# A transformer-block kernel's first row block: first loads, an early split on ScalarE and GpSimd, and another first order of the products

## The chip, the cores and the metric

The kernel runs on one core of a Trainium2 chip. The metric is the device time of one execution in microseconds (us). Each core has a matrix engine (TensorE, PE in the profile, with its weight loads as PEld), a vector engine (VectorE, DVE), a scalar engine (ScalarE, ACT), a general engine (GpSimd, POOL) and a queue engine that issues DMAs (SyncE, SP).

## The reference, cut to what matters

```
x: 2048 x 640;  w1: 640 x 1536;  w2: 1536 x 640
xn = (x - mean(x)) / sqrt(var(x) + 1e-5)          # by row
a, b = xn @ dft_hid_re.T, xn @ dft_hid_im.T
A = dft_seq_re @ a - dft_seq_im @ b               # 2048 x 2048 matrices
B = gelu(xn @ w1 + b1) @ w2 + b2
out = x + A + B
```

All data are float32. The change touches only the start of B for the first 512 rows: the layer norm, the transposition of the normalized rows, and the first products with `w1`.

## The kernel before

The work goes in four blocks of 512 rows (`TB`), each of four chunks of 128 rows (`NC` = 4), and the hidden dimension of 1536 in twelve chunks of 128 columns (`NF`). The input dimension of 640 makes five pieces of 128 (`ND`, index `j`).

Every float32 operand of a product is split in two float32r parts: a high part, which is a rounded copy that ScalarE writes (`high`, line 186), and a low part, which is the difference that VectorE writes (`low`, line 189). A product of two split operands is three matmuls: high by high, high by low and low by high. `split` (lines 176 to 183) makes both parts.

`hidden(g)` (lines 308 to 323) computes one chunk of the hidden layer for one block: fifteen matmuls into one PSUM bank, a step (j, k) for each of the five pieces `j` and three kinds `k`. Kind 0 is high by high, kind 1 takes the high part of `W1` with the low part of the rows (`XT`), and kind 2 takes the low part of `W1` with the high part of the rows. The first chunk (g = 0) takes its steps in the order of the list `FIRST`; the second (g = 1) has its kind 2 steps last.

The schedule is written out by hand: each engine runs its instructions in the order of the program. There is no planner. Loads go through the queue of SP in that order too; an instruction in that queue that waits holds back those behind it. Tiles of one tag share a few places (`bufs=3` for `w1r` and `w2r`), so that a load waits until the last reader of the tile that held its place is done.

The start of the kernel, in program order:

- SP loads the four row chunks (`load_x`, line 208), then chunks 0 and 1 of `w1` (`load_w1`, line 278, four DMAs each), then chunk 2 of `w1`, chunk 0 of `w2` (`load_w2`, line 285), the bias `b1c`, and chunks 1 and 2 of `w2`.
- VectorE fills three tiles `warm` with zeros, and PE runs 19 matmuls on them into a bank that is not read (`NWARM`, line 666). The three tiles share the places of `w1r`, so the first loads of `w1` wait for the matmuls that read the tile.
- The four chunks are normalized in different ways. Chunk 0: VectorE takes mean and variance (lines 215 and 216), ScalarE the root (690), VectorE the reciprocal and one step of Newton's method (700 to 702, 708, 709), and ScalarE writes the normalized chunk (714). Chunk 1 (`last`): ScalarE takes mean and square sum (692 to 699) and scales it at the end (721). Chunks 2 and 3: VectorE takes the statistics, ScalarE one root for chunks 1 to 3 (707), VectorE the steps behind it (710 to 713), and VectorE normalizes (236) in two pieces for each chunk: columns of pieces 0 and 1, then of 2 to 4.
- ScalarE makes the high part of the first `w1` chunk (723) and VectorE its low part (734).
- PE transposes 20 squares of 128 x 128 into five banks `tacc` (682): those of chunk 0, then pieces 0 and 1 of chunks 2 and 3, all of chunk 1, and the rest; the last one stands behind the first product.
- ScalarE and VectorE split each of the five banks into `XT[j]` (186 and 189).
- PE runs the rest of `hidden(0)`, then `hidden(1)`, which needs the second `w1` chunk (`prep_w1(1)`), and goes on with further chunks and with the products with `w2` (lines 300 to 302).

Of the kernel before, what the change touches and what calls it, by code (L numbers as in the profile page):

```python
# [10 lines left out]
F32 = mybir.dt.float32  # L11
F32R = mybir.dt.float32r
AF = mybir.ActivationFunctionType
ALU = mybir.AluOpType

P = 128
Q = 4
B = 32
EPS = 1e-5
NWARM = 19  # L20
NGATE = (7, 10)
TAIL = 4
PADL = 8
# [3 lines left out]
def kernel(  # L27
# [45 lines left out]
    nc = tc.nc  # L73
    x = x.flatten_outer_dims()
    out = out.flatten_outer_dims()
    S, D = x.shape
    F = w1.shape[1]
    TB = 512
# [3 lines left out]
    ND = D // P  # L82
# [4 lines left out]
    NC = TB // P  # L87
# [4 lines left out]
    def pool(name, side="left", stack=ctx):  # L92
        return stack.enter_context(tc.tile_pool(name=name, bufs=1, side=side, reuse_waits="tile"))
# [22 lines left out]
    def bank(k):  # L116
        return banks[:, k]
# [4 lines left out]
    b1c = const.tile([P, NF], F32, name="b1c")  # L122
    b2c = const.tile([P, ND], F32, name="b2c")
    eps = const.tile([P, 2], F32, name="eps")
    MV = const.tile([P, 4, 6], F32, name="mv")
# [6 lines left out]
    early = pool("early", stack=es_e)  # L132
# [18 lines left out]
    slots = {}  # L151
# [33 lines left out]
    def high(h, s):  # L185
        nc.scalar.activation(h, s, AF.Copy)  # L186
# [17 lines left out]
    def load_x(c, eng=nc.sync, k=None, home=None):  # L204

        slot[c] = c % NC if k is None else k
        xt[c] = (row_places if home is None else home)[:, slot[c]]
        eng.dma_start(xt[c], x[c * P : (c + 1) * P])  # L208

    def ln_stats(c):  # L210
        m = MV
        st = ST[c % 2]
        half = D // 2
        for h in range(2):
            nc.vector.bn_stats(st[:, h, :], xt[c][:, h * half : (h + 1) * half])  # L215
        nc.vector.bn_aggr(m[:, slot[c], 0:2], st.rearrange("p a b -> p (a b)"))  # L216
# [37 lines left out]
    def zo_tile(name, shape=(P, NB, DQ), dtype=F32):  # L254
        return out_pool.tile(list(shape), dtype, tag="zo", bufs=1, name=name)
# [8 lines left out]
    W1, W2, w1r, w2r = {}, {}, {}, {}  # L264
# [4 lines left out]
    def load_w1(i, eng=nc.sync):  # L269

        if i >= 3 * NF:
            return
        f0 = (i % NF if i < 2 * NF else AGAIN[i - 2 * NF]) * P
        t = early.tile([P, ND, P], F32, tag="w2r" if i == NF + 5 else "w1r", bufs=3, name=f"w1r{i}")
        w1r[i] = t
        v = w1.rearrange("(q c i) f -> q i c f", q=Q, i=B)
        for q in range(Q):
            eng.dma_start(t[q * B : (q + 1) * B], v[q, :, :, f0 : f0 + P])

    def load_w2(i, eng=nc.sync):  # L280
        if i >= NF:
            return
        t = early.tile([P, D], F32, tag="w2r", bufs=3, name=f"w2r{i}")
        w2r[i] = t
        eng.dma_start(t, w2[i * P : (i + 1) * P, :])

    def prep_w1(i, n=None):
        if i < NF:
            W1[i] = slots[1, i]
            split(W1[i][:, 0], W1[i][:, 1], w1r.pop(i if n is None else n).rearrange("p a b -> p (a b)"))  # L290

    def prep_w2(i):
        if i < NF:
            W2[i] = slots[2, i]
            split(W2[i][:, 0], W2[i][:, 1], w2r.pop(i), perm=True)
# [12 lines left out]
    def hidden(g, part=slice(None)):  # L308
        i = g % NF
        acc = bank((5 if g < NF else 0) + g % 3)  # L310
        kinds = ((0, 0), (0, 1), (1, 0))
        steps = [(j, k) for j in range(ND) for k in range(3)]
        if g == 0:
            steps = FIRST
        if g == 1:

            steps.sort(key=lambda s: s[1] == 2)
        for n, (j, k) in list(enumerate(steps))[part]:
            a, b = kinds[k]
            nc.tensor.matmul(  # L320
                acc, W1[i][:, a, j * P : (j + 1) * P], XT[j][:, b], start=n == 0, stop=n == len(steps) - 1
            )
        return acc
# [24 lines left out]
        low(hs[:, 1], a, hs[:, 0])  # L348


    FIRST = [(0, 0), (0, 2), (1, 0), (1, 2), (0, 1), (2, 0), (2, 2), (1, 1), (3, 0), (3, 2)]
    FIRST += [(2, 1), (4, 0), (4, 2), (3, 1), (4, 1)]

    def gelu(g, acc, fill=lambda k: None):

# [290 lines left out]

    zeros = rows.tile([P, TB], F32, tag="yt", bufs=2, name="zeros")

    warms = [early.tile([P, TB], F32R, tag="w1r", bufs=3, name=f"warm{k}") for k in range(3)]

    for c in range(NC):
        load_x(c)
    nc.gpsimd.memset(eps, EPS)
    make_identity(nc, ident)
    nc.vector.memset(zeros, 0.0)
# [1 line left out]
        nc.vector.tensor_copy(warm, zeros)  # L657

    nc.scalar.activation(eps[:, 1:2], eps[:, 0:1], AF.Sqrt)
    load_w1(0)  # L660
    load_w1(1)

    wacc = bank(5)
    for k in range(NWARM):
        warm = warms[sum(k >= n for n in NGATE)]
        nc.tensor.matmul(wacc, warm[:, :P], warm, start=True, stop=True)
    load_w1(2)
    load_w2(0)
    nc.sync.dma_start(b1c, b1.rearrange("(i p) -> p i", p=P))
    load_w2(1)  # L670
    load_w2(2)

# [5 lines left out]
    xp = zo_tile("xp", (P, NC, D))  # L678

    def transpose_x(c, j0, j1):  # L680
        for j in range(j0, j1):
            nc.tensor.transpose(tacc[j][:, c * P : (c + 1) * P], xp[:, c, j * P : (j + 1) * P], ident)  # L682
# [4 lines left out]
    f, m = MV[:, 0], MV[:, last]  # L687
# [9 lines left out]
        bias=m[:, 5:6],  # L697
# [2 lines left out]
    nc.vector.reciprocal(root, root)  # L700
    nc.vector.scalar_tensor_tensor(step, root, -0.5, root, op0=ALU.mult, op1=ALU.mult)
    nc.vector.scalar_tensor_tensor(step, f[:, 1:2], EPS, step, op0=ALU.add, op1=ALU.mult)
    for c in (2, 3):
        ln_stats(c)
    others = MV[:, 1:NC]
    v, r, t = others[:, :, 1], others[:, :, 3], others[:, :, 4]
    nc.scalar.activation(r, v, AF.Sqrt, bias=eps[:, 0:1])  # L707
    nc.vector.scalar_tensor_tensor(root, step, 1.5, root, op0=ALU.add, op1=ALU.mult)  # L708
    nc.vector.scalar_tensor_tensor(shift, f[:, 0:1], -1.0, root, op0=ALU.mult, op1=ALU.mult)
    nc.vector.reciprocal(r, r)  # L710
    nc.vector.scalar_tensor_tensor(t, r, -0.5, r, op0=ALU.mult, op1=ALU.mult)
    nc.vector.scalar_tensor_tensor(t, v, EPS, t, op0=ALU.add, op1=ALU.mult)
    nc.vector.scalar_tensor_tensor(r, t, 1.5, r, op0=ALU.add, op1=ALU.mult)
    nc.scalar.activation(  # L714
        chunked(xp[:, 0]),
        xt[0].rearrange("p (q c i) -> p q c i", q=Q, i=B),
# [1 line left out]
        bias=shift,  # L718
        scale=root,
    )  # L720
    nc.scalar.activation(xp[:, last], xp[:, last], AF.Copy, scale=m[:, 3:4])
    W1[0], first_w1 = slots[1, 0], w1r.pop(0).rearrange("p a b -> p (a b)")
    nc.scalar.activation(W1[0][:, 0], first_w1, AF.Copy)

    for j0, j1 in ((0, 2), (2, ND)):
        for c in (2, 3):
# [4 lines left out]
    transpose_x(last, 0, ND)  # L731
    transpose_x(2, 2, ND)
    transpose_x(3, 2, ND - 1)
    nc.vector.tensor_tensor(W1[0][:, 1], first_w1, W1[0][:, 0].bitcast(F32), op=ALU.subtract)
    for j in range(ND):
        split(XT[j][:, 0], XT[j][:, 1], tacc[j])
        if j == 0:
            hidden(0, slice(0, 1))
            transpose_x(3, ND - 1, ND)
# [6 lines left out]
    A["rows_a"] = rows_in("rt2")  # L746
    for c in range(NC, 2 * NC):
        load_x(c, home=A["rows_a"])
    acc0 = hidden(0, slice(1, None))
    prep_w1(1)  # L750
    acc1 = hidden(1)
    prep_w2(0)
    prep_w1(2)
    load_w2(3)
# [937 lines left out]
    for kind, what in stages:  # L1692
        b = blocks.index(what) if kind == "s" else b
# [24 lines left out]
    t = blocks[-2][1]  # L1718
# [38 lines left out]
```

## Time and profile before

| | us |
|---|---|
| median of 3 runs | 852.09 |
| lowest and highest of them | 851.99, 852.13 |
| span of the profiled execution | 849.94 |

The profiled execution's own time is not recorded beside its span; the median stands 2.15 us above the span.

| engine | busy us | share of the span | instructions |
|---|---|---|---|
| PE | 841.9 | 99% | 3711 |
| PEld | 696.7 | 82% | 3711 |
| DVE | 686.7 | 81% | 909 |
| ACT | 368.6 | 43% | 527 |
| POOL | 67.7 | 8% | 116 |

Times in the trace are us from the start of the span. Busy time counts the stretches in which an instruction of the engine runs; matmuls overlap one another, so their starts, not their lengths, give the pace. A row such as `11.03 2.56 ACT L186 ... x5` tells that five instructions of line 186 ran on ScalarE one after another from 11.03 for 2.56 us. A lower-case q behind an engine's name (SPq) is its queue of DMA issues.

### The profile page before, as it was taken

The numbers are of one execution on the slowest core, as the hardware profiler recorded it, in microseconds if no ns is written. First come the engines' busy times: TensorE is split into PE (matmuls) and PEld (weight loads), VectorE is DVE, ScalarE is ACT, GpSimd is POOL, SyncE is SP. The second block draws the span as 40 slices with busy tenths as digits, with TensorE's granted clock in tenths as the row PEclk, the third lists the DMA queues.
The fourth block names the chain that finished last, engine by engine and source line by source line (L and its number), as shares of the span: only waits on it lengthen the run. The fifth ranks groups of instructions, "written<-read, shape, count | busy, mean of one in ns | idle before, by whom it ended". The sixth has DMA issues, their size and how long they took to land.

```text
span 849.9 us, 10599 instructions
## 1 busy us (share of the span) xinstructions
PE 841.9 (99%) x3711; PEld 696.7 (82%) x3711; DVE 686.7 (81%) x909; ACT 368.6 (43%) x527; POOL 67.7 (8%) x116
## 2 busy tenths in 40 slices
PE   8999999999999999999999999999999999999997
PEld 7888888888888888888888888888888888888886
DVE  7979889767844778979978887889967998885687
ACT  7655666654453555443444344232323433323241
POOL 0440024222301000000000000000000000000002
PEclk9999999999999999999999999999999999999999
DMA  8995667878977897958744679763745799705464
GB/s 230 288 248 158 139 163 250 260 223 305 262 192 199 333 323 138 209 120 193 158 137 107 167 220 283 165 144 99 214 150 156 229 237 234 303 19 180 124 172 108
DMA packets 199141, 166.53 MB, mean 196 GB/s; under 512 B 61648, under 2 KB 170192, under 8 KB 198576
## 3 DMA queue, kind: packets, MB, share of 16 engines
q1 hardware_dynamic: 188320, 140.42, 62.7%
q0 software_dynamic: 7600, 24.91, 8.7%
q10 hardware_dynamic: 3168, 0.52, 0.3%
q8 instruction: 29, 0.48, 0.2%
q14 instruction: 24, 0.20, 0.1%
HBM read 115.75 MB, written 46.14 MB: 190 GB/s over the span
## 4 chain that ended last, share of the span: by engine, by line
PE 98%; DMA 1%; DVE 0%; ACT 0%; SPq 0%; issue 0%; ACTq 0%
PE banks L301 29%; PE banks L302 29%; PE banks L300 29%; PE banks L320 10%; DMA row<-in_A_x_dram 1%; PE banks L682 0%; DVE st L215 0%; ACT xp L714 0%; SPq L208 0%; DVE yo L1722 0%; DVE mv L216 0%; ACT mv L707 0%; DVE mv L708 0%; ACTq L707 0%
## 5 line engine op out<-in xcount | busy, mean ns | idle before, releaser
L186 ACT ACTIVATE as<-r 128x1024 fp32r<-128x1024 f32 x80 | 85.0, 1062 | 171.1 <-PE banks L302 150.4
L300 PE MATMUL banks<-as,xab 128*128 128x512 f32 x407 | 158.3, 389 | 0.0
L302 PE MATMUL banks<-as,xab 128*128 128x512 f32 x407 | 158.3, 389 | 0.0
L301 PE MATMUL banks<-as,xab 128*128 128x512 f32 x407 | 158.3, 389 | 0.0
L189 DVE TENSOR_TENSOR as<-r,as 128x1024 fp32r<-128x1024 f32 x80 | 97.2, 1215 | 38.1 <-ACT as L186 38.0
L301 PEld LDWEIGHTS banks<-as,xab 128*128 128x128 f32 x407 | 76.4, 188 | 15.9
L302 PEld LDWEIGHTS banks<-as,xab 128*128 128x128 f32 x407 | 76.4, 188 | 15.8
L300 PEld LDWEIGHTS banks<-as,xab 128*128 128x128 f32 x407 | 76.4, 188 | 15.8
L300 PE MATMUL banks<-as,xc 128*128 128x512 f32 x224 | 87.1, 389 | 0.0
L301 PE MATMUL banks<-as,xc 128*128 128x512 f32 x224 | 87.1, 389 | 0.0
L302 PE MATMUL banks<-as,xc 128*128 128x512 f32 x224 | 87.1, 389 | 0.0
L186 ACT ACTIVATE as<-rt 128x1024 fp32r<-128x1024 f32 x32 | 34.0, 1063 | 72.5 <-PE banks L302 57.9
L320 PE MATMUL banks<-xt,xab 128*128 128x512 f32 x240 | 56.8, 390 | 0.0
L189 DVE TENSOR_TENSOR hs<-ab,hs 128x512 fp32r<-128x512 f32 x36 | 24.7, 685 | 37.6 <-ACT hs L186 37.6
L320 PEld LDWEIGHTS banks<-xt,xab 128*128 128x128 f32 x240 | 45.0, 188 | 9.4
L301 PEld LDWEIGHTS banks<-as,xc 128*128 128x128 f32 x224 | 42.1, 188 | 8.8
L302 PEld LDWEIGHTS banks<-as,xc 128*128 128x128 f32 x224 | 42.0, 188 | 8.7
L300 PEld LDWEIGHTS banks<-as,xc 128*128 128x128 f32 x224 | 42.1, 188 | 8.7
L1280 POOL DMA_DIRECT2D out_dram<-u x4 | 2.6, 658 | 568.8 <-DVE u L463 568.8
L302 PE MATMUL banks<-hs,xc 128*128 128x512 f32 x120 | 46.7, 389 | 0.0
L300 PE MATMUL banks<-hs,xc 128*128 128x512 f32 x120 | 46.7, 389 | 0.0
L301 PE MATMUL banks<-hs,xc 128*128 128x512 f32 x120 | 46.7, 389 | 0.0
(240 smaller groups left out, 1678.9 us busy)
## 6 DMA issues: line engine op xcount, KB each, us to landing
raw<-in_A_dft_seq_re_dram SPq DMA_DIRECT2D x64, 256.0 KB, 5.4
raw<-in_A_dft_seq_im_dram SPq DMA_DIRECT2D x64, 256.0 KB, 5.1
w1r<-in_B_w_dram SPq DMA_DIRECT2D x144, 80.0 KB, 3.5
wit<-wst POOLq DMA_DIRECT2D x15, 384.0 KB, 4.2
wit<-wst POOLq DMA_DIRECT2D x20, 256.0 KB, 4.5
forms_ab<-xab SPq DMA_DIRECT2D x4, 1280.0 KB, 7.7
xab<-wit SPq DMA_DIRECT2D x13, 384.0 KB, 4.5
row<-xn SPq DMA_DIRECT2D x14, 320.0 KB, 5.3
```

Of the source, the lines that this page charges most:

```text
L186: nc.scalar.activation(h, s, AF.Copy)
L189: nc.vector.tensor_tensor(l, s, h.bitcast(F32), op=ALU.subtract)
L300: nc.tensor.matmul(acc, wh, mh, start=first, stop=False, skip_group_check=goes_on)
L301: nc.tensor.matmul(acc, wh, ml, start=False, stop=False, skip_group_check=goes_on)
L302: nc.tensor.matmul(acc, wl, mh, start=False, stop=last, skip_group_check=goes_on)
L320: nc.tensor.matmul(acc, W1[i][:, a, j * P : (j + 1) * P], XT[j][:, b], start=n == 0, stop=n == len(steps) - 1)
L1280: queues[q % len(queues)].dma_start(rows_of(out, t)[:, :, q * DQ + c0 : q * DQ + c1], src[q * B : (q + 1) * B])
```

## The change

- The three `warm` tiles take the places of `w2r`, so that no load of `w1` waits for them, and the loads of `w1`'s chunks 0 to 2 are issued right behind the rows. The bias is loaded ahead of `w2`. One warm matmul less runs (18).
- Chunk 0's last two VectorE steps and ScalarE's write of it stand ahead of the statistics of chunks 2 and 3.
- ScalarE makes the high part of the first `w1` chunk ahead of the scaling of chunk 1.
- GpSimd, and not VectorE, makes the low part of the first `w1` chunk. Ahead of it stands a GpSimd copy of one column of chunk 3's normalized rows into `eps[:, 1:2]`, which nothing reads afterwards; it waits for the last of VectorE's normalizing instructions.
- The list `FIRST` has the first kind 2 step in seventh place and not in second. The second chunk's steps are sorted by kind: all of kind 0, of kind 1, of kind 2.
- The last two steps of the first chunk, (3, 1) and (4, 1), run after the five kind 0 steps of the second chunk.

```diff
-NWARM = 19
+NWARM = 18
...
-            steps.sort(key=lambda s: s[1] == 2)
+            steps.sort(key=lambda s: s[1])
...
-    FIRST = [(0, 0), (0, 2), (1, 0), (1, 2), (0, 1), (2, 0), (2, 2), (1, 1), (3, 0), (3, 2)]
-    FIRST += [(2, 1), (4, 0), (4, 2), (3, 1), (4, 1)]
+    FIRST = [(0, 0), (1, 0), (0, 1), (2, 0), (1, 1), (3, 0), (0, 2), (1, 2), (4, 0), (2, 1)]
+    FIRST += [(2, 2), (3, 2), (4, 2), (3, 1), (4, 1)]
...
-    warms = [early.tile([P, TB], F32R, tag="w1r", bufs=3, name=f"warm{k}") for k in range(3)]
+    warms = [early.tile([P, TB], F32R, tag="w2r", bufs=3, name=f"warm{k}") for k in range(3)]
     for c in range(NC):
         load_x(c)
+    for i in range(3):
+        load_w1(i)
...
-    load_w1(0)
-    load_w1(1)
...
-    load_w1(2)
+    nc.sync.dma_start(b1c, b1.rearrange("(i p) -> p i", p=P))
     load_w2(0)
-    nc.sync.dma_start(b1c, b1.rearrange("(i p) -> p i", p=P))
...
     nc.vector.scalar_tensor_tensor(step, f[:, 1:2], EPS, step, op0=ALU.add, op1=ALU.mult)
-    for c in (2, 3):
-        ln_stats(c)
-    others = MV[:, 1:NC]
-    v, r, t = others[:, :, 1], others[:, :, 3], others[:, :, 4]
-    nc.scalar.activation(r, v, AF.Sqrt, bias=eps[:, 0:1])
     nc.vector.scalar_tensor_tensor(root, step, 1.5, root, op0=ALU.add, op1=ALU.mult)
     nc.vector.scalar_tensor_tensor(shift, f[:, 0:1], -1.0, root, op0=ALU.mult, op1=ALU.mult)
-    nc.vector.reciprocal(r, r)
...
     nc.scalar.activation(
         chunked(xp[:, 0]),
...
+    for c in (2, 3):
+        ln_stats(c)
+    others = MV[:, 1:NC]
+    v, r, t = others[:, :, 1], others[:, :, 3], others[:, :, 4]
+    nc.scalar.activation(r, v, AF.Sqrt, bias=eps[:, 0:1])
+    W1[0], first_w1 = slots[1, 0], w1r.pop(0).rearrange("p a b -> p (a b)")
+    high(W1[0][:, 0], first_w1)
+    nc.vector.reciprocal(r, r)
...
     nc.scalar.activation(xp[:, last], xp[:, last], AF.Copy, scale=m[:, 3:4])
-    W1[0], first_w1 = slots[1, 0], w1r.pop(0).rearrange("p a b -> p (a b)")
-    nc.scalar.activation(W1[0][:, 0], first_w1, AF.Copy)
...
-    nc.vector.tensor_tensor(W1[0][:, 1], first_w1, W1[0][:, 0].bitcast(F32), op=ALU.subtract)
+    nc.gpsimd.tensor_copy(eps[:, 1:2], xp[:, 3, D - 1 :])
+    nc.gpsimd.tensor_tensor(W1[0][:, 1], first_w1, W1[0][:, 0].bitcast(F32), op=ALU.subtract)
...
-    acc0 = hidden(0, slice(1, None))
     prep_w1(1)
-    acc1 = hidden(1)
+    hidden(0, slice(1, -2))
+    hidden(1, slice(0, ND))
+    acc0 = hidden(0, slice(-2, None))
+    acc1 = hidden(1, slice(ND, None))
```

More of the change, by code (lines that the diff above doesn't have):

```diff
@@ L702 @@
     nc.vector.scalar_tensor_tensor(step, f[:, 1:2], EPS, step, op0=ALU.add, op1=ALU.mult)
-    for c in (2, 3):
-        ln_stats(c)
-    others = MV[:, 1:NC]
-    v, r, t = others[:, :, 1], others[:, :, 3], others[:, :, 4]
-    nc.scalar.activation(r, v, AF.Sqrt, bias=eps[:, 0:1])
     nc.vector.scalar_tensor_tensor(root, step, 1.5, root, op0=ALU.add, op1=ALU.mult)
     nc.vector.scalar_tensor_tensor(shift, f[:, 0:1], -1.0, root, op0=ALU.mult, op1=ALU.mult)
-    nc.vector.reciprocal(r, r)
-    nc.vector.scalar_tensor_tensor(t, r, -0.5, r, op0=ALU.mult, op1=ALU.mult)
-    nc.vector.scalar_tensor_tensor(t, v, EPS, t, op0=ALU.add, op1=ALU.mult)
-    nc.vector.scalar_tensor_tensor(r, t, 1.5, r, op0=ALU.add, op1=ALU.mult)
     nc.scalar.activation(
@@ L720 @@
     )
+    for c in (2, 3):
[6 more added lines that the diff above has]
+    nc.vector.reciprocal(r, r)
+    nc.vector.scalar_tensor_tensor(t, r, -0.5, r, op0=ALU.mult, op1=ALU.mult)
+    nc.vector.scalar_tensor_tensor(t, v, EPS, t, op0=ALU.add, op1=ALU.mult)
+    nc.vector.scalar_tensor_tensor(r, t, 1.5, r, op0=ALU.add, op1=ALU.mult)
     nc.scalar.activation(xp[:, last], xp[:, last], AF.Copy, scale=m[:, 3:4])
-    W1[0], first_w1 = slots[1, 0], w1r.pop(0).rearrange("p a b -> p (a b)")
-    nc.scalar.activation(W1[0][:, 0], first_w1, AF.Copy)
     for j0, j1 in ((0, 2), (2, ND)):
```

## The prediction

> **What bounds the kernel now.** I read the page's chain of waits first: PE holds 98% of it. The chain in order of time, cut to the first 30 us, shows what comes ahead of PE (columns: start, length, what; us).
>
> ```profile
> 1.67 4.54 DMA row<-in_A_x_dram
> 6.23 0.90 DVE st L215 x2
> 7.36 0.76 DVE st L215 x2
> 8.66 0.91 ACT xp L714
> 9.71 2.27 PE banks L682 x19
> 12.32 10.07 PE banks L320 x44
> ```
>
> The third row chunk lands at 1.67 + 4.54 = 6.21, its statistics and the fourth's follow on DVE, then ScalarE writes `xp[0]`, PE transposes, and the first 44 hidden products run without a hole: 10.07 / 44 = 0.229 us each. The table of windows says that no hole follows either (columns: length, then busy us of PE, PEld, DVE, ACT, POOL, clock, DMA share, GB/s):
>
> ```profile
> 22.40:844.50 822.10, 822.10 (x3627) 680.58 (x3626) 669.76 (x870) 352.09 (x499) 66.89 (x109) 1.00 0.72 195
> ```
>
> PE is busy 822.10 of 822.10 us. So the change can only shift the moment at which the product stream starts, or open holes in its first products; each passes to the end one to one. The timeline gives the first block (start, busy us, engine, line; the three single rows are narrow windows).
>
> ```profile
> 0.75 1.82 SPq L208 DMA_DIRECT2D row<-in_A_x_dram  x4
> 1.06 0.29 POOL masks.py:199 TENSOR_SCALAR_AFFINE_SELECT ident<-ident 128x128 f32<-128x128 f32 x1
> 1.92 7.05 PE L666 MATMUL banks<-warm 128*128 128x512 f32 x19 [1.92 <-DVE warm L657]
> 5.31 5.60 SPq L278 DMA_DIRECT2D w1r<-in_B_w_dram  x12
> 5.62 0.16 DVE L702 SCALAR_TENSOR_TENSOR mv<-mv 128x1 f32<-128x1 f32 x1
> 7.45 0.19 ACT L699 ACTIVATION_READ_ACCUMULATOR scratch<-xp 128x1 f32 x1
> 8.14 0.21 DVE L216 BATCH_NORM_AGGREGATE mv<-st 128x2 f32<-128x12 f32 x1
> 8.45 0.30 ACT L707 ACTIVATE mv<-mv,eps 128x3 f32<-128x3 f32 x1 [0.81 <-DVE mv L708]
> 9.40 0.17 DVE L713 SCALAR_TENSOR_TENSOR mv<-mv 128x3 f32<-128x3 f32 x1
> 9.60 0.83 ACT L721 ACTIVATE xp<-xp,mv 128x640 f32<-128x640 f32 x1
> 9.60 1.51 DVE L236 TENSOR_SCALAR xp<-row,mv 128x256 f32<-128x256 f32 x4
> 9.60 0.41 DVE L236 TENSOR_SCALAR xp<-row,mv 128x256 f32<-128x256 f32 x1
> 9.93 0.41 DVE L236 TENSOR_SCALAR xp<-row,mv 128x256 f32<-128x256 f32 x1
> 10.33 0.72 ACT L723 ACTIVATE xab<-w1r 128x640 fp32r<-128x640 f32 x1
> 11.03 2.56 ACT L186 ACTIVATE xt<-banks 128x512 fp32r<-128x512 f32 x5
> 11.09 0.82 DVE L734 TENSOR_TENSOR xab<-w1r,xab 128x640 fp32r<-128x640 f32 x1
> 11.73 0.48 PE L320 MATMUL banks<-xt,xab 128*128 128x512 f32 x1
> 11.83 3.07 DVE L189 TENSOR_TENSOR xt<-banks,xt 128x512 fp32r<-128x512 f32 x5
> 12.04 0.27 PE L682 MATMUL banks<-ident,xp 128*128 128x128 f32 x1
> 12.07 10.32 PE L320 MATMUL banks<-xt,xab 128*128 128x512 f32 x44
> 12.87 0.63 PE L320 MATMUL banks<-xt,xab 128*128 128x512 f32 x2
> ```
>
> And means of one from the groups by form:
>
> ```profile
> L189 DVE TENSOR_TENSOR xt<-banks,xt 128x512 fp32r<-128x512 f32 x5 | 3.1, 680 | 0.0
> L186 ACT ACTIVATE xt<-banks 128x512 fp32r<-128x512 f32 x5 | 2.6, 608 | 0.0
> L320 PE MATMUL banks<-xt,xab 128*128 128x512 f32 x240 | 56.8, 390 | 0.0
> ```
>
> From these: a transpose every (2.27 - 0.27) / 18 = 0.111 us; a ScalarE high part of `xt` every (2.56 - 0.61) / 4 = 0.49; a VectorE low part every (3.07 - 0.68) / 4 = 0.60; and from the end of a high part (11.03 + 0.61 = 11.64) to the product that uses it (11.73) 0.09, which I call 0.1.
>
> **The change part by part.** *First row chunk early.* The two DVE steps for chunk 0 move ahead of the statistics of chunks 2 and 3. They fit behind L702 (ends 5.78): two of about 0.2 end at 6.17, before row 2 lands at 6.21, so the statistics lose nothing. ScalarE's write of `xp[0]` then starts when L699 ends, 7.64, not 8.66, and takes 0.91: 8.55. The Sqrt of the other chunks, at 8.45 before, waits for the fourth chunk's statistics, which end at 8.35 as before; it slips by 0.1 at most, since ScalarE started L714 0.21 after the start of that Sqrt and so overlaps neighbours. I take nothing and keep 0.1 for the range. L713 still ends at 9.57, and L236 and L721 still start at 9.60.
>
> *What early `xp[0]` buys.* Its five transposes go at about 8.65, one pitch after the warm stream, which is one product (0.23) shorter. In the old order the 19 transposes were one dense run from 9.71, and the nineteenth started at 9.71 + 18 x 0.111 = 11.71, just when the first high part was ready. In the new order the remaining fourteen follow L236: its first piece ends at 10.01, so chunk 2's first pair starts at 10.11; the second ends at 10.34, so chunk 3's pair starts at 10.44 and 10.55; chunk 1's first, whose `xp` is ready at 10.43, at 10.66; nine more bring the nineteenth to 11.66. Chunk 1's first was the tenth of the dense run, at 10.71. So 0.54 us of transposes leaves the path, but L236 and L721 are late next, and 0.05 is left of it.
>
> *The first chunk of `w1`.* Its high part moves ahead of L721 on ScalarE: from 8.66 (behind the Sqrt) it takes 0.72, to 9.38, within the wait for L713. That holds if the chunk has landed by about 8.85. Its four loads now stand right behind the rows on SP (2.57 instead of 5.31), and before, issued from 5.31, they took
>
> ```profile
> L278 SPq DMA_DIRECT2D w1r<-in_B_w_dram x4: 332/438/438, 5.3 to 6.6; - x4
> DMA to landing us min/median/max: 2.1/2.2/2.5
> ```
>
> So the last of them landed at about 6.6 + 2.2 = 8.8. Of the four rows the same view says
>
> ```profile
> DMA to landing us min/median/max: 3.0/4.0/4.9
> ```
>
> which puts the last row, issued at about 2.1, at 7.0. Queued behind rows that land at 6.21 and 7.0, I expect `w1` at 7.5 to 8.3: an estimate, half a chunk's time and more behind them. Removing L723 behind L721 frees ScalarE at 10.43 instead of 11.05, but the high part of `xt[0]` then waits for chunk 1's first transpose: 11.03 - 0.05 = 10.98. The first product starts at 11.68 instead of 11.73.
>
> *L734 leaves DVE.* The low parts of `xt` start when the first high part is there, about 11.63, rather than 11.83. That is 0.2 us, but no product waited for them.
>
> *L734's work goes to GpSimd.* It stands behind a one-column copy that waits for the last L236 (9.60 + 1.51 = 11.11), so it starts at about 11.3. The trace has no GpSimd two-input operation. Its bounds are 0.82 (VectorE's row, were the engines equal) and 2.9: the 128-column select, 0.29, scaled by columns is 5 x 0.29 = 1.45, doubled for a second input. I take 1.45, the same engine's row, and so 12.75. By the Trainium skill (GPSIMD Engine Reference, 3.1, measured numbers: a two-input add over 2,048 columns takes 4,497 ns against 2,293 on VectorE) the estimate is 640 x 2.2 ns = 1.4 us; by it the sum stays, by the 2.9 it grows by 0.9. The same page (4.1) advises against plain elementwise work there, and no run so far has such a row.
>
> *The new first order.* The old one alternated (0,0),(0,2),(1,0),(1,2): two products for each high part, 0.46 against ScalarE's 0.49. The new one puts `W1`'s low part (k = 2) seventh and relies on low parts of `xt` earlier. High parts are usable at 11.68, 12.17, 12.66 and 13.15, low parts at 11.63 + 0.68 + 0.1 = 12.41, then 13.01. So: (0,0) 11.68, the transpose, (1,0) 12.17 (waits 0.1), (0,1) 12.41, (2,0) 12.66, (1,1) 13.01 (waits 0.12), (3,0) 13.24. The old sixth product starts at 12.87 + 0.63 - 0.39 = 13.11. So this order gives back 0.05 and 0.13 more. The seventh needs GpSimd's low part at 13.47; at 12.75 + 0.1 it is there with 0.6 to spare. From then on high and low parts are ahead of the stream (the next tight one, (2,1) at 14.16, has its part at 13.61).
>
> *Two chunks interleaved.* Holding back (3,1) and (4,1) behind five products of chunk 1 needs that chunk's high part at 15.07, and the later ones need its low part at 17.8:
>
> ```profile
> 13.52 0.77 ACT L186 ACTIVATE xab<-w1r 128x640 fp32r<-128x640 f32 x1
> 14.82 0.81 DVE L189 TENSOR_TENSOR xab<-w1r,xab 128x640 fp32r<-128x640 f32 x1
> 16.95 0.69 ACT L340 ACTIVATE ab<-banks,b1c 128x512 f32<-128x512 f32 x1
> 18.34 0.69 DVE L189 TENSOR_TENSOR hs<-ab,hs 128x512 fp32r<-128x512 f32 x1 [1.24 <-ACT hs L186]
> 22.23 0.39 PE L300 MATMUL banks<-hs,xc 128*128 128x512 f32 x1
> ```
>
> They are there at 14.3 and 15.6. The first accumulator is complete at about 16.8, ahead of its GELU at 16.95, and the `hs` made from it is first used at 22.23 after standing ready at 19.03: 3 us of cover. Without it, the cost would be what the GELU slips.
>
> *Queues.* On SP the bias and `w2` loads move ahead with `w1`; the fourth `w1` chunk now waits for GpSimd (12.75) instead of L734 and is issued no later than about 13.2. GpSimd's next instruction is a store long after. Nobody waits for these.
>
> **The sum.** -0.05 for the start, +0.18 for the two waits: +0.13. The profiled execution spans 849.94 us, so 850.07; the median, 852.09, lies 2.15 above the span, hence 852.2. A measurement of this kernel tells about 0.2% (1.7 us) from no change, and this is far inside it. Faster by that much is hardly open: all that PE does not fill lies ahead of 11.73, and it hangs on rows landing at 6.21 that the change does not bring sooner.
>
> **Rivals.** *GpSimd late (slower).* The seventh product waits at PE's head of queue, and all behind it. It decides from an operation longer than 13.47 - 0.1 - 11.3 = 2.07 us, us for us: 2.9 gives 852.2 + 0.85 = 853.0, and past 0.2% needs 3.7. For it: no row of such an operation, and a first use. Against: 1.45 by the select's row.
>
> *GpSimd blocks VectorE.* If both cannot run together, the low part of `xt[0]` starts at 12.75, not 11.63: the third product slips by 1.1, to 853.3; the length from which this passes 0.2% is 2.0. For it: only that the operation is held until L236 is over. Against: VectorE's L189 takes one input from PSUM. The Trainium skill (SBUF — State Buffer, Who interferes with whom) says that an exclusive port lock holds between GpSimd and a VectorE instruction with two SBUF inputs, and not one with a single SBUF input; by that rule this rival is out for the `xt` low parts. No run so far shows it.
>
> *Row landings move.* `w1`'s packets run on the same engines as rows 2 and 3. If row 2 lands later the whole chain follows us for us; at most one chunk's share, half of the 8.8 - 6.2 between them, 1.3, to 853.5. Or `w1` lands past 8.85 and pushes L721 likewise. Against: the rows are ahead in the queue.
>
> *Clock lost.* PE now idles from about 9.2 to 10.1, 0.9 us against 0.74 (8.97 to 9.71). The nineteen warm products took 7.05 us, far above 19 x 0.229 = 4.35: PE begins slow. A fallback costs about the same 2.7 us: 854.9. Against: the 0.74 gap was followed by full pace. The Trainium skill (TensorE: Matmul & The Clock Gate, What's actually happening) puts the fallback at an idle window of about 3.4 us; by that it stays away, as the trace agrees for 0.74.
>
> **How the numbers follow.** My forecast, within -0.4 to +0.6: 0.62. GpSimd late 0.20, of which 0.05 past 0.2%. GpSimd blocking 0.08, 0.03 past it. Rows 0.06. Clock 0.04, all past it. So slower 0.12, faster 0.01, same 0.87. The range runs from 851.7 (the forecast with its unknowns in our favour) to 853.2, which takes in GpSimd at 2.9; what is left out is below 0.2.
>
> **What would show it.** Right: transposes in two groups, near 8.65 and from 10.1; first product near 11.68; small holes at the second and fifth product; a GpSimd operation of about 1.45 us ending before 13.4; PE busy without holes afterwards. Wrong: a hole at the seventh product ending at GpSimd, low parts of `xt` starting after GpSimd ends, row 2 landing later than 6.3, or products at 0.43 us after 11.7.

## The result, and the profile after

The changed kernel takes 853.04 us in the median of 21 runs (851.83 to 855.09), the kernel before 851.99 in 21 runs beside it (851.29 to 853.93). The ratio is 1.0015, interval 1.0008 to 1.0021: slower by about 1.3 us (0.7 to 1.8). The forecast was 852.2 and no change that can be told; the time lies inside its range, but the change did cost more than the runs leave uncertain.

The runs themselves already say something that the median doesn't. Of the 21, nine lie from 851.83 to 852.42, five from 852.71 to 853.42 and seven from 853.96 to 855.09. Before, one of 21 lies above 853.5. So nine of them lost little, five about 1 us, and a third lost 2 to 3 us.

The profiled execution is one of those that lost little: its span is 850.2, against 849.94. Its chain of waits in order of time (start, length, what; us), cut to the first 30 us:

```profile
2.13 5.32 DMA row<-in_A_x_dram
7.47 0.90 DVE st L215 x2
8.70 0.31 ACT mv L714
9.85 0.42 DVE xp L236
10.32 1.86 PE banks L680 x14
12.53 10.26 PE banks L320 x44
```

Before, the chain went through the third row chunk, landing at 6.21. Now it goes through the fourth (2.13 + 5.32 = 7.45), which before landed at about 7.0 and was on no path. The DMA view of the four row loads (time from issue to landing) shows the same: 4.9 at most before, and now

```profile
DMA to landing us min/median/max: 3.0/3.8/5.3
```

Behind the first block nothing changed; in the table of windows PE still has no hole (columns as before):

```profile
22.40:844.70 822.30, 822.30 (x3629) 680.85 (x3627) 670.28 (x870) 351.90 (x499) 66.73 (x109) 1.00 0.71 195
```

The timeline of the first block (start, busy us, engine, line; in brackets the idle time before it and what ended it; the last row is from a narrow window, and holds the fifth to seventh product):

```profile
7.47 0.89 DVE L215 BATCH_NORM_STATS2 st<-row 128x6 f32<-128x320 f32 x2 [0.20 <-DMA row<-in_A_x_dram]
7.61 0.91 ACT L703 ACTIVATE xp<-row,mv 128x640 f32<-128x640 f32 x1
8.66 0.74 PE L680 MATMUL banks<-ident,xp 128*128 128x128 f32 x5 [0.43 <-ACT xp L703]
8.90 0.72 ACT L186 ACTIVATE xab<-w1r 128x640 fp32r<-128x640 f32 x1
9.85 1.52 DVE L236 TENSOR_SCALAR xp<-row,mv 128x256 f32<-128x256 f32 x4
10.32 1.86 PE L680 MATMUL banks<-ident,xp 128*128 128x128 f32 x14 [0.92 <-DVE xp L236]
11.75 1.56 POOL L733 TENSOR_TENSOR xab<-w1r,xab 128x640 fp32r<-128x640 f32 x1
11.86 1.89 DVE L189 TENSOR_TENSOR xt<-banks,xt 128x512 fp32r<-128x512 f32 x3 [0.49 <-ACT xt L186]
11.93 0.48 PE L320 MATMUL banks<-xt,xab 128*128 128x512 f32 x1
12.37 10.41 PE L320 MATMUL banks<-xt,xab 128*128 128x512 f32 x44
13.20 0.96 PE L320 MATMUL banks<-xt,xab 128*128 128x512 f32 x3
```

VectorE now waits for the fourth chunk's load. Its statistics start at 7.47, L236 at 9.85 and the first product at 11.93, where 11.68 was forecast. The price of the new order came out as forecast: from the first product's start to the start of the last of the 44 are 12.37 + 10.41 - 0.39 - 11.93 = 10.46 us, against 12.07 + 10.32 - 0.39 - 11.73 = 10.27. Its holes stand elsewhere: the trace has 0.44, 0.34 and 0.34 us from start to start ahead of the second, third and sixth product, where waits at the second and fifth were forecast.

### The profile page after: what moved, and what is told of

Same layout as the page of the kernel before. It is cut to its first block, busy times and chain, and to the rows that moved or that the text cites. A ratio compares the mean times of both kernels' runs of the same rounds, so it can differ in the third digit from the quotient of the medians.

```text
span 850.2 us, 10600 instructions
## 1 busy us (share of the span) xinstructions
PE 841.7 (99%) x3710; PEld 696.1 (82%) x3710; DVE 686.3 (81%) x908; ACT 368.3 (43%) x527; POOL 69.5 (8%) x118
## 4 chain that ended last, share of the span: by engine, by line
PE 98%; DMA 1%; DVE 0%; SPq 0%; issue 0%; ACT 0%; ACTq 0%
PE banks L301 29%; PE banks L300 29%; PE banks L302 29%; PE banks L320 10%; DMA row<-in_A_x_dram 1%; PE banks L680 0%; SPq L208 0%; DVE st L215 0%; DVE yo L1723 0%; DVE xp L236 0%; ACT mv L714 0%; DVE mv L216 0%; DVE mv L717 0%; DVE mv L720 0%; DVE mv L719 0%
```

## The experiments

All times are medians over five rounds, each beside runs of the kernel before on the same chip: 851.71 (33 runs) for the first four kernels, 851.98 (32) for the next four, 851.59 (33) for the last four.

### The changed kernel again, and with its hole filled

The first suspicion was PE's clock. `e1_after` is the changed kernel as it is.

> The changed kernel once more, beside the runs below. Of its 21 timed executions 8 took 851.83 to 852.25 us, 7 took 853.96 to 855.09, and the mean granted clock was 0.997 or 0.998 in most of the latter against 0.999. Theory C (clock): in some executions PE falls back to half its clock around the hole between chunk 0's transposes and the rest, for one or two of the 3.41 us steps in which the clock is set; so again about a third of the executions above 853.5, with a lower mean clock, and a lower edge near 851.9. Rival R (every execution pays the same: row 3 landing 0.4 later and the first products waiting, about +0.4): executions in one group near the median, within 0.5 us, and no tie between time and clock.

Measured: 852.48 (851.82 to 854.78, 11 runs), ratio 1.0015 (1.0006 to 1.0024). The loss is confirmed. Two of the eleven lie above 853.5, at 854.66 and 854.78, and both have a mean granted clock of 0.997, the other nine 0.998 to 1.0. In its profile the rows happened to land early, the fourth at 6.92:

```profile
11.63 0.48 PE L320 MATMUL banks<-xt,xab 128*128 128x512 f32 x1
```

That is the 11.68 of the forecast within 0.05. So the arithmetic of the start held in this execution; how late the rows land changes from one execution to the next.

`e2_fill` is the changed kernel with PE kept busy between the first transposes and the others:

```diff
-NWARM = 18
+NWARM = 19
...
-    load_w2(2)
...
     transpose_x(0, 0, ND)
+    for k in range(4):
+        nc.tensor.matmul(wacc, warms[2][:, :P], warms[2], start=True, stop=True)
+    load_w2(2)
```

> The changed kernel with 19 instead of 18 warm products ahead of chunk 0's transposes and four more behind them, in the hole of 1.07 us. Nothing else moves but the third load of w2, which waits for them. Theory C: no execution above 853.5, median 852.0 to 852.4, some 0.4 above the kernel before. Rival R: the same distribution as the changed kernel, median near 853.0, since filler products take nothing off the rows or the order.

Measured: 852.38 (852.00 to 853.03, 11 runs), ratio 1.001 (1.0001 to 1.0019). None lies above 853.5, although the rows landed later in its profile than in that of the changed kernel (the fourth at 8.08). Its PE rows:

```profile
9.33 1.18 PE L727 MATMUL banks<-warm 128*128 128x512 f32 x4
10.95 1.85 PE L679 MATMUL banks<-ident,xp 128*128 128x128 f32 x14 [0.45 <-DVE xp L236]
```

With the hole down to 0.45 us the long executions are gone; a loss of about 0.7 us stays. These were the first sign of two parts: a late start, and a clock that is lost in some executions.

### A hole alone, and the first row chunk alone

`e3_short` is the kernel before with `NWARM = 15` in place of 19.

> The kernel before with 15 instead of 19 warm products: a hole of some 1.6 us instead of 0.73 ahead of its transposes, and not one useful instruction moved. Theory C: a part of the executions, a quarter or more, 1 to 3 us above the rest, so that the median rises by 0.2 to 1.5. Rival R: the same time as before within 0.1 us, since nothing useful waits for a warm product.

Measured: 851.64 (851.16 to 853.04, 11 runs), ratio 0.9999 (0.999 to 1.0008). A quarter or more of long executions was expected, and there was none above 853.5; one, at 853.04, has a clock of 0.997. PE's hole ahead of the transposes was

```profile
9.64 2.27 PE L682 MATMUL banks<-ident,xp 128*128 128x128 f32 x19 [1.49 <-ACT xp L714]
```

1.49 us. With the old loads a hole of that size cost at most this one execution of eleven its clock. The clock theory alone had missed.

`e4_early` is the kernel before with the change's early normalization of chunk 0 and nothing else:

```diff
     nc.vector.scalar_tensor_tensor(step, f[:, 1:2], EPS, step, op0=ALU.add, op1=ALU.mult)
-    for c in (2, 3):
-        ln_stats(c)
...
     nc.vector.scalar_tensor_tensor(root, step, 1.5, root, op0=ALU.add, op1=ALU.mult)
...
+    for c in (2, 3):
+        ln_stats(c)
```

> The kernel before with one part of the change alone: chunk 0's last two steps and its write ahead of the statistics of chunks 2 and 3. Its transposes go near 8.9 and leave a hole of about 0.9 us behind them. Theory C: a part of the executions 1 to 3 us longer, fewer than in the changed kernel as its holes are smaller (19 warm products). Rival R: -0.1 to +0.1 us in every execution, since the rows land as before and the order of the products is the old one.

Measured: 851.67 (851.33 to 852.29, 11 runs), ratio 1.0001 (0.9993 to 1.001). It neither gains nor loses anything that can be told.

### The loads alone, and all the rest without them

`e5_loads` is the kernel before with the change's loads only:

```diff
-    warms = [early.tile([P, TB], F32R, tag="w1r", bufs=3, name=f"warm{k}") for k in range(3)]
+    warms = [early.tile([P, TB], F32R, tag="w2r", bufs=3, name=f"warm{k}") for k in range(3)]
...
+    for i in range(3):
+        load_w1(i)
...
-    load_w1(0)
-    load_w1(1)
...
-    load_w1(2)
```

> The kernel before with one part of the change alone: the warm tiles in the places of w2r and the three w1 chunks loaded right behind the rows. Theory L (loads): w1's packets delay the rows; rows 2 and 3 land up to 1 us later than 6.2 and 7.0 and by a different amount in each execution, so the median rises by 0.3 to 0.8 us and the spread by as much. Theory C (clock) adds: when the rows are late, PE's hole ahead of the transposes grows, and single executions come out 2 to 3 us longer. Rival R (the order of the first products and GpSimd's operation carry the shift): within 0.1 us of the kernel before.

`e6_noloads` is the changed kernel with the old loads, the same lines the other way round.

> The changed kernel with the old loads: warm tiles in the places of w1r, w1 issued after the first warm products. Theory L: rows land at 6.2 and 7.0 again, the median is 0.1 to 0.3 us above the kernel before (what the new order gives back), and no execution is above 853.5. Theory C without L (the hole behind chunk 0's transposes is enough): a quarter of the executions still above 853.5. Rival R: as the changed kernel's lower edge, some 0.4 above the kernel before.

Measured: `e5_loads` 853.23 (852.29 to 855.46, 12 runs), ratio 1.0018 (1.0009 to 1.0027), five of twelve above 853.5. `e6_noloads` 852.19 (851.64 to 852.86, 11 runs), ratio 0.9999 (0.9991 to 1.0008), none above 853.5. The loads alone carry the whole loss, and all other parts together cost nothing that can be told. The DMA view of the rows, first of `e5_loads`, then of `e6_noloads`:

```profile
DMA to landing us min/median/max: 3.0/4.0/5.9
```

```profile
DMA to landing us min/median/max: 3.0/3.6/4.3
```

The rows are issued at the same times in both. With the loads right behind them in the queue the last of them lands 1.6 us later (7.99 against 6.41). The DMA view counts the packets between 2 us and that landing, again `e5_loads` first:

```profile
DMA packets 1446, 1.68 MB, mean 281 GB/s; under 512 B 139, under 2 KB 951, under 8 KB 1446
DMA packets 592, 1.29 MB, mean 293 GB/s; under 512 B 64, under 2 KB 93, under 8 KB 592
```

Packets of `w1` hold 512 bytes, those of the rows 2560. So 951 - 139 = 812 packets of `w1`, more than the 640 of a whole chunk, were under way before the last row packets had landed, and 93 - 64 = 29 with the old loads. Transfers that stand behind the rows in the queue do pass the last packets of the rows.

### Late rows and a hole together

`e7_short_after` is the changed kernel with `NWARM = 15`: the edit of `e3_short`, which cost nothing there, in the company of the early loads.

> The changed kernel with 15 instead of 18 warm products, so that 0.7 us more of PE's time ahead of chunk 0's transposes is idle. Theory C: more executions than in the changed kernel above 853.5, half or more, with a mean clock of 0.997, and a profile that catches one shows the granted clock at 0.5 for about 3.4 or 6.8 us within the first 17 us. Theory L alone: the same distribution as the changed kernel (9 of 32 above 853.5, median 852.5 to 853.0).

Measured: 854.72 (852.25 to 855.56, 9 runs), ratio 1.003 (1.002 to 1.004), eight of nine above 853.5. Here the profile caught a long execution (span 853.7). Rows, statistics and transposes, from the DMA view and the timeline:

```profile
DMA to landing us min/median/max: 3.1/4.8/7.2
```

```profile
8.73 0.74 PE L680 MATMUL banks<-ident,xp 128*128 128x128 f32 x5 [1.18 <-ACT xp L703]
9.37 0.89 DVE L215 BATCH_NORM_STATS2 st<-row 128x6 f32<-128x320 f32 x2 [0.32 <-DMA row<-in_A_x_dram]
12.21 2.84 PE L680 MATMUL banks<-ident,xp 128*128 128x128 f32 x14 [2.74 <-DVE xp L236]
14.70 0.78 PE L320 MATMUL banks<-xt,xab 128*128 128x512 f32 x1
```

The fourth row chunk lands at 9.35, and PE stands idle 2.74 us ahead of the fourteen transposes, which take 2.84 instead of 1.86; the first product takes 0.78 instead of 0.48. The table of windows, cut at the steps of the granted clock (third column from the end), says why:

```profile
6.06:9.47 3.41, 2.23 (x12) 1.41 (x10) 1.40 (x6) 2.47 (x4) 0.00 (x0) 1.00 0.75 172
9.47:12.89 3.42, 0.68 (x5) 0.56 (x6) 2.82 (x11) 1.75 (x3) 0.00 (x0) 1.00 0.48 129
12.89:16.30 3.41, 3.41 (x15) 3.08 (x14) 2.45 (x5) 2.51 (x5) 1.73 (x2) 0.50 0.94 227
16.30:19.70 3.40, 3.40 (x16) 2.76 (x15) 3.30 (x5) 3.38 (x6) 0.00 (x0) 1.00 0.94 285
```

In the window from 9.47 PE was busy 0.68 of 3.42 us, and in the next the clock is 0.50. One step at half pace costs about 3.41 / 2 = 1.7 us, an estimate; then the clock returns. The profile bears it out: its span is 3.5 us longer than the changed kernel's (853.7 against 850.2), its fourteen transposes start 12.21 - 10.32 = 1.9 later because of the rows, and 1.6 is left. So the late rows cost this execution as much as the clock. In the changed kernel's own profile the same cut gives

```profile
9.53:12.95 3.42, 2.63 (x19) 2.20 (x19) 2.85 (x8) 2.64 (x6) 1.39 (x2) 1.00 0.81 126
```

with PE busy 2.63 us, and no fall behind it.

### The order alone

`e8_order` is the kernel before with the new `FIRST`, the new sorting and the interleaving of the two chunks; VectorE still makes the low part of `w1`.

```diff
-    FIRST = [(0, 0), (0, 2), (1, 0), (1, 2), (0, 1), (2, 0), (2, 2), (1, 1), (3, 0), (3, 2)]
...
+    FIRST = [(0, 0), (1, 0), (0, 1), (2, 0), (1, 1), (3, 0), (0, 2), (1, 2), (4, 0), (2, 1)]
...
-    acc0 = hidden(0, slice(1, None))
...
+    hidden(0, slice(1, -2))
+    hidden(1, slice(0, ND))
```

> The kernel before with one part of the change alone: the new order of the first chunk's steps and the interleaving with the second chunk; w1's low part stays on VectorE. By the forecast's schedule the first six products wait 0.1 to 0.2 more: +0.1 to +0.25 in every execution, no long tail. VectorE still makes w1's low part ahead of the low parts of xt, so (0,1) in third place waits longer, up to 0.2 more than in the changed kernel: +0.3 at most. Rival R (the order carries all of the 0.5 to 1 us): +0.5 or more.

Measured: 852.37 (851.53 to 853.06, 11 runs), ratio 1.0004 (0.9995 to 1.0012), none above 853.5. In time it isn't told from nothing. Its timeline

```profile
11.24 0.48 PE L320 MATMUL banks<-xt,xab 128*128 128x512 f32 x1
11.68 10.58 PE L320 MATMUL banks<-xt,xab 128*128 128x512 f32 x44
```

gives 11.68 + 10.58 - 0.39 - 11.24 = 10.63 us, 0.36 above before and a little over what was expected.

### Which loads, how many, how late

`e9_wide` is the kernel before with other loads right behind the rows: two chunks of `w2`, while `w1` stays where it was.

```diff
     for c in range(NC):
         load_x(c)
+    for i in range(2):
+        load_w2(i)
...
-    load_w2(0)
...
-    load_w2(1)
```

> The kernel before with the first two w2 chunks loaded right behind the rows, in place of the w1 chunks, which keep their old time. They are as many bytes (320 KB a chunk) in packets of 2560 B, each DMA over all 128 partitions, where a w1 DMA has 160 packets of 512 B to 32 partitions. Theory L1 (what delays the rows is how w1's packets meet the last row packets): rows land as in the kernel before, rows 2 and 3 at 5.5 to 6.2 and 6.3 to 7.1. Theory L2 (any bytes behind the rows delay them): row 3 at 7.4 or later. The time says less, since w1 now lands behind 640 KB more: +0.2 to +1 us by either.

Measured: 852.71 (851.68 to 854.56, 11 runs), ratio 1.0014 (1.0005 to 1.0023), three above 853.5. The fourth row chunk landed at 7.50. That is not particular to `w1`'s loads: other transfers behind the rows make them late too. The time of this kernel says less, since `w1` now lands behind `w2` and its high part starts at 10.95 instead of 10.33:

```profile
10.95 0.74 ACT L723 ACTIVATE xab<-w1r 128x640 fp32r<-128x640 f32 x1 [0.21 <-DMA w1r<-in_B_w_dram]
```

`e10_half` is as `e5_loads`, but only `w1`'s chunk 0 stands right behind the rows; chunks 1 and 2 follow later, behind `w2`'s first.

```diff
+    load_w1(0)
...
-    load_w1(0)
-    load_w1(1)
-
...
+    load_w2(0)
+    load_w1(1)
     load_w1(2)
-    load_w2(0)
```

> The kernel before with the first w1 chunk alone right behind the rows (in the changed kernel the second is under way too before row 3 lands). Theory L with a cost for each byte behind the rows: row 3 later than 7.1, but by less than with three chunks, median +0.2 to +0.8. Rival (only the second chunk's packets, which start while rows 2 and 3 are still coming, do harm): rows and median as in the kernel before, within 0.2.

Measured: 853.54 (851.80 to 855.61, 11 runs), ratio 1.0023 (1.0013 to 1.0032), six above 853.5. That a third of the bytes would do less harm was wrong. The profile is again of a long execution (span 852.8), and shows the same steps; its transposes start 11.02 - 9.71 = 1.3 us later than in the kernel before, and the other 1.6 of its 2.9 us more are again about one step at half clock:

```profile
DMA to landing us min/median/max: 2.9/4.4/6.4
```

```profile
11.02 3.38 PE L681 MATMUL banks<-ident,xp 128*128 128x128 f32 x19 [2.98 <-ACT xp L713]
```

```profile
8.57:11.99 3.42, 0.97 (x9) 1.00 (x10) 3.00 (x13) 2.19 (x4) 0.00 (x0) 1.00 0.59 150
11.99:15.40 3.41, 3.41 (x16) 3.13 (x15) 2.99 (x6) 2.64 (x6) 0.00 (x0) 0.50 0.90 187
```

`e11_late` goes the other way, the kernel before with its loads later still: `NGATE = (9, 12)` in place of (7, 10).

> The kernel before with its w1 loads held back longer: the warm tiles are read by 9 and 12 products instead of 7 and 10, so w1's first issue goes from 5.3 to about 6.15. Theory L carried on: if the old loads too cost the rows something, rows 2 and 3 land at 5.6 and 6.4 more often and the median falls by 0.1 to 0.4 us; w1 then lands at about 9.6, still ahead of its use on ScalarE at 10.33. Rival: the old loads are already clear of the rows, 0 +- 0.1.

Measured: 851.59 (851.36 to 852.16, 11 runs), ratio 1.0001 (0.9992 to 1.001). The old place of the loads was already clear of the rows; nothing is to be had there.

`e12_long_loads` is `e5_loads` with `NWARM = 23`, so that PE is busy until the transposes.

> The kernel with the early loads alone (5 of 12 executions above 853.5, median 853.23) with 23 instead of 19 warm products, which fill 0.9 us of the hole ahead of the transposes. Theory C: executions above 853.5 become fewer, 1 of 11 at most, and the median falls to 852.5 to 853.0; the landing of the rows stays as late. Theory L alone (late rows are the whole of it): the same distribution as with 19, or worse, as PE is still warming when rows come early.

Measured: 852.32 (851.78 to 855.04, 11 runs), ratio 1.0009 (1.0 to 1.0018). Ten of eleven are at or below 852.47 and one at 855.04, where `e5_loads` had five of twelve above 853.5. The hole is all but gone in its profile, with the fourth row chunk still late (7.34):

```profile
9.85 2.26 PE L680 MATMUL banks<-ident,xp 128*128 128x128 f32 x19 [0.24 <-ACT xp L712]
```

## Why the prediction was wrong, and where it was right

The steps that failed are two rivals that the prediction took as separate and put at 0.06 and 0.04, with nothing for either in the sum: *row landings move* and *clock lost*. They are one chain. Loads queued right behind the rows make the last row land later; statistics and L236 follow; PE's hole ahead of the transposes grows; and where it falls into a step of the clock so that PE does too little in it, the clock goes to half for 3.41 us.

How often the clock fell can be read from the mean granted clock of each execution. A step at half clock takes 3.41 / 2 / 852 = 0.002 from it. The twelve profiles without such a step have 0.998 to 1.000, the two with one 0.997. So 0.997 tells of a lost step, 0.999 and more rule one out, and 0.998 leaves it open. By what was in the kernel:

| | executions above 853.5 | mean clock 0.997 |
|---|---|---|
| old loads (`e3_short`, `e4_early`, `e6_noloads`, `e8_order`, `e11_late`) | 0 of 55 | 1 of 55 |
| kernel before, all its runs | 2 of 119 | 0 of the 98 whose clock is on record |
| early loads (the changed kernel twice, `e5_loads`, `e9_wide`, `e10_half`) | 23 of 66 | 13 of 66 |
| early loads, PE's hole wider (`e7_short_after`) | 8 of 9 | 8 of 9 |
| early loads, PE's hole filled (`e2_fill`, `e12_long_loads`) | 1 of 22 | 1 of 22 |

The limit of 853.5 mixes the two parts. Five of the 23 long executions, from 853.54 to 853.96, have a clock of 0.999 or more; they lost no step, and the late start is what is left for them. The one of `e3_short` that lost a step stayed below the limit at 853.04, 1.4 above its kernel's median. So each half can occur without the other, but early loads and an unfilled hole together make nearly all long executions. Of the loss, the thirteen executions of the changed kernel with 0.999 or more average 0.6 us above the kernel before, and all 21 average 1.2. So about half of it is there without the clock, and the rest comes with the executions that may have lost a step. With the hole filled 0.7 us stay in both kernels, which fits.

Step by step:

- *"The rows are ahead in the queue."* This was the argument against the first rival, and it is false as a protection. With old loads the fourth row chunk landed between 6.34 and 7.04 in six profiles, with early loads between 6.92 and 9.35 in eight. The prediction's bound for a later landing was 1.3 us; the latest of these is 2.3 behind the profile before. Its sign for this rival, row 2 (the third chunk) later than 6.3, did not show in the changed kernel's profile, where that chunk landed at 5.96: it was the fourth, which the prediction left at 7.0, that came late.
- *"The 0.74 gap was followed by full pace."* True, and it told nothing of a gap of 2.7 us. The prediction sized PE's idle time from the rows landing at 6.21 and 7.0, as they did in one execution, and so had 0.9.
- *"The statistics lose nothing"* leaned on a margin of 0.04 us from that same execution. In `e6_noloads` the third row chunk landed at 5.63 and the moved steps stood in the way:

```profile
6.04 0.16 DVE L704 SCALAR_TENSOR_TENSOR mv<-mv 128x1 f32<-128x1 f32 x1
6.11 0.88 DVE L215 BATCH_NORM_STATS2 st<-row 128x6 f32<-128x320 f32 x2
```

L704 is the second of them, and the statistics start 0.48 us behind the landing. The first product starts at 11.60; in `e8_order`, with its rows at 5.55 and 6.34 and these steps in the old place, it starts at 11.24. So where rows land early the moved steps lose 0.36 us instead of nothing. `e4_early`, where the first row chunk landed 0.3 us earlier and the steps were done sooner, shows no cost in time, at 0.1% of uncertainty.
- *The start of the products*, -0.05, was +0.20 in the profile (11.93), all of it from the late row; `e1_after`, with its rows at 5.77 and 6.92, had -0.10 (11.63).
- *The new order*, +0.18, was +0.19.
- *The 2.15 us from span to time* were the median of some runs less the span of another. Where an execution has both, the time stands 1.72 to 1.82 above the span in the 21 of the changed kernel, and 1.76 to 2.11 in the kernel before. By span the median execution took 851.3 where the sum had 850.07, so 1.2 us more; about 0.4 of that was hidden by the 2.15.
- *What a measurement tells* was taken as 0.2% (1.7 us). The interval of the 21 runs is about 0.55 us either way, so a loss of 1.3 is told.
- *GpSimd*, taken at 1.45 us, took 1.56 (L733) and ended at 13.31. The seventh product started at 13.20 + 0.96 - 0.39 = 13.77, 0.23 behind the sixth (13.54 in the trace) as in a dense stream, so the rival of a late GpSimd is out. The estimate from the Trainium skill's figures (GPSIMD Engine Reference, 3.1) had been 1.4.
- *GpSimd blocks VectorE* is out too: low parts of `xt` started at 11.86 while it ran, and every (1.89 - 0.68) / 2 = 0.60 us, as before. The rule of the Trainium skill (SBUF — State Buffer, Who interferes with whom) agrees.
- *Interleaving and the queues* cost nothing, as forecast: PE has no hole from 22.40 on, and `e6_noloads`, which has the interleaving, is at 0.9999.

That the time lies inside the range is luck: it had been stretched to 853.2 for a GpSimd operation of 2.9 us, not for what happened.

## What to carry to other kernels

A transfer that isn't urgent should not be queued right behind one on the critical path: standing ahead in the queue did not keep the rows' landing time. Here the old place of the loads lost nothing. A margin of a twentieth of a microsecond read from one execution is no margin, so look at the landings in several profiles. Where a start depends on them, filling PE's hole ahead of the first real work with products that nobody reads took away nearly all long executions here, though not the 0.7 us of the late start.

## What the runs showed of the hardware

The granted clock changes in steps of 3.41 us, and it fell to 0.50 behind steps in which PE was busy 20% (0.68 of 3.42, `e7_short_after`) and 28% (0.97 of 3.42, `e10_half`). At 77% (2.63 of 3.42, the changed kernel) it stayed, and at 57% in `e3_short`:

```profile
7.38:10.80 3.42, 1.93 (x15) 1.48 (x14) 2.99 (x13) 2.48 (x6) 0.00 (x0) 1.00 0.64 169
```

Where between 28% and 57% the line is was not tried, nor whether the share is what counts. In both steps that fell PE ran nothing but transposes, while the step of `e3_short` also holds 0.77 us of warm products (they end at 8.15), and in all fourteen profiles every other step of the first block, from the first at a clock of 1.00 on, holds at least that much of products. It may be that transposes don't count. Then the stretch from the last warm product to the first product decides: it is 7.15 us in `e7_short_after` and 6.0 in `e10_half`, 3.3 to 3.7 in the other profiles with early loads and no filling, 3.5 in `e3_short`, 2.1 to 3.1 in the others with old loads, and 2.0 and 2.3 with the hole filled. Only a stretch of more than 3.41 can hold a whole step, which fits the counts above. No run separates the two readings.

The Trainium skill (TensorE: Matmul & The Clock Gate, What's actually happening) tells of the fallback for an idle window of about 3.4 us. The length agrees; the rest agrees only if a window with nothing but transposes counts as idle. The prediction set a gap of 0.9 us against it, which took the transposes for work and the rows as on time, and so the clock rival looked safe. The steps stand at different places of the span in different executions (one ends at 9.47 in `e7_short_after` and at 8.57 in `e10_half`), which fits that only some executions fall; that it decides which ones was not tried by itself.

Left open: how packets that stand later in the queue come to pass the last row packets, since loads of `w2` make the rows late as those of `w1` do, and one chunk as well as three; and how far the landings spread for one and the same kernel, since each kernel has only one or two profiles.
